# Transposing the second piece of v by DMA in a fused attention and FFN kernel, with later loads of w3, finer first folds and a split last piece of k

One core of a Trainium2 chip (trn2). The metric is the time of one execution in microseconds on the device; lower is better. The span that a profile shows is about 1.8 us less than that time.

## The reference

```python
# q, k, v: (4, 5824, 256) float32; tau = 1; w1, w2: (256, 1024); w3: (1024, 1024); w_out: (1024, 256)
qn = q / (norm(q, axis=1) + 1e-6)
kn = k / (norm(k, axis=1) + 1e-6)
s  = kn.transpose(0, 2, 1) @ qn / tau            # a 256 x 256 score matrix for each batch
a  = softmax(s)
x  = (v @ a).reshape(23296, 256)
h  = (x @ w1) * (x @ w2) @ w3
out = h @ w_out
```

## The kernel before

The kernel folds the softmax matrix into w1 and w2 for each batch (`Wf`), and w3 with w_out into one matrix `W` once. What is left for each batch is: for each chunk of 512 tokens and each of 8 slices j, products a and b (of `Wf` with the transposed v), `as` (ACT's copy of a), `abs = as * b` (VectorE), and o (TensorE, `abs` with `W`). TensorE works in program order here (below it stands for 3.4 us in front of chunk 6, with o products behind it that it could have run). While `W` isn't there yet, only a, b and `abs` run, and the `abs` wait in buffers: the 16 of chunks 0 and 1 in four free q buffers, the rest in a pool of 34.

```python
    def transpose_piece(n, pi):                     # by DMA, SBUF to SBUF, on SP's queue
        ...
        nc.sync.dma_start_transpose(vT[:, pi * PIECE : (pi + 1) * PIECE, :, :], t[:, :, :])

    def gate():                                     # POOL waits until VectorE is as far as this
        nc.gpsimd.tensor_copy(gate_t, last_ab[0][:1, :1])
    def hold(src):                                  # POOL waits until src is written; it issues all loads
        nc.gpsimd.tensor_copy(gate_t, src)

    # in emit_ab: where abs goes
            if b == 0 and c < 2:
                if j % 4 == 0:
                    held[0] = in_pool.tile([P, 4, 512], BF16, tag="q", ...)
                ab = held[0][:, j % 4, :]
            else:
                ab = work.tile([P, 512], BF16, tag="ab_sb", ..., bufs=8 * NDEF + 2)     # 34

    # loads of batch 0, in order
    load_piece("k", 0, 5)
    ...
    load_piece("q", 0, 5, (1, 3, 4)); load_part("v", 0, 0, 0, half)
    # w1 and w2 in three steps, then
    load_part("v", 0, 0, half, PIECE); load_piece("v", 0, 1); load_piece("v", 0, 2)
    nc.gpsimd.dma_start(out=wout_sb, ...)
    nc.gpsimd.dma_start(out=w3_bf, in_=w3r)

    # the agenda of batch 0: at(time on TensorE's own clock, its cost, what)
            at(4.6, 0.5, lambda: transpose_half_on_pe(0, 0, 1, False))
            at(7.0, 0.5, lambda: transpose_half_on_pe(0, 1, 0, True))      # v piece 1, on TensorE
            at(8.0, 0.5, lambda: transpose_half_on_pe(0, 1, 1, False))
            at(15.0, 0.0, transpose_w3)                                    # four DMA transposes
            at(15.0, 0.0, lambda: transpose_piece(0, 2))
            for jt in range(FT):
                at(27.5 + 1.2 * jt, 0.87, lambda jt=jt: w_unit(jt))
            moves = [("qk", 1, 0, 29.0), ("v", 0, 3, 30.0), ("v", 0, 4, 30.5), ("qk", 1, 1, 44.0), ...]
            t0, t1 = 54.0, 113.0                    # the score units of batch 1 lie between these
```

## Time and profile before

| | kernel before |
|---|---|
| time, median of 6 runs | 569.5 us (569.38 to 569.57) |
| span of the profiled run, mean granted TensorE clock | 567.7 us, 0.999 |
| TensorE busy | 557.6 us, 98% |
| first product a | 37.27 us |
| chunk 2, chunk 6 begin (need v pieces 1 and 3) | 55.4, 106.6 us |
| waits of TensorE after the first a | none |

How to read the views: PE is TensorE (PEld its weight loads), DVE is VectorE, ACT ScalarE, POOL GpSimd and SP SyncE; a timeline line of SPq or POOL with a DMA shows the issue of transfers, not their landing. A wait line says who waited, for whom, and then the total in us, the number of times and the longest. A timeline line has start and length in us, the engine, the line of the kernel, the operation, and in brackets how long the engine had been idle and what ended that. Line numbers differ by one or two between the kernels.

### The profile page before, as it was taken

To read this page: it belongs to the slowest core of one execution; us is meant where nothing else is said; L and a number is where in the kernel's file an instruction comes from. 1 tells how busy PE (TensorE), PEld (TensorE's weight loads), DVE (VectorE), ACT (ScalarE), POOL (GpSimd) and SP (SyncE) were. 2 spreads that over 40 slices of the span, in tenths; PEclk is the share of its full clock that TensorE was granted. 3 is DMA by queue.
4 is the path that set the end of the run, shared out by engine and by line. 5 is a ranking of instruction groups with operands and counts; after the bars stand their busy time and mean duration, and the time that the engine had idled before them with its cause. 6 is when DMAs were issued, how large, how long until landed. Compare 5 with 4: busy or idle time off the path is not lost.

```text
span 567.7 us, 10095 instructions
## 1 busy us (share of the span) xinstructions
PE 557.6 (98%) x3755; PEld 355.4 (63%) x3755; DVE 375.4 (66%) x581; ACT 338.7 (60%) x627; POOL 77.9 (14%) x163
## 2 busy tenths in 40 slices
PE   8799999999999999999999999999999999999997
PEld 5664566776656666666656566666655655665655
DVE  1047645888966577888766668787876665565564
ACT  1057536777766577777675567777765554454453
POOL 4260013120111111121210101030120000000000
PEclk9999999999999999999999999999999999999999
DMA  9999989978455796595661595765740325221011
GB/s 213 211 182 209 173 171 237 226 164 192 115 142 121 143 192 148 90 193 123 145 149 75 97 219 117 155 120 121 185 112 39 85 74 149 64 68 71 38 70 61
DMA packets 75104, 77.45 MB, mean 136 GB/s; under 512 B 54192, under 2 KB 58800, under 8 KB 75056
## 3 DMA queue, kind: packets, MB, share of 16 engines
q0 software_dynamic: 15760, 38.93, 39.3%
q1 hardware_dynamic: 59008, 37.23, 22.0%
q10 hardware_dynamic: 288, 0.66, 0.4%
q8 instruction: 29, 0.48, 0.3%
q14 instruction: 19, 0.16, 0.1%
HBM read 78.91 MB, written 23.86 MB: 181 GB/s over the span
## 4 chain that ended last, share of the span: by engine, by line
PE 93%; DMA 5%; ACT 1%; POOL 0%; issue 0%; DVE 0%; ACTq 0%; POOLq 0%
PE o L521 28%; PE b L476 28%; PE a L476 28%; PE G L192 5%; DMA k<-in_k_dram 5%; PE fold L363 2%; PE w L649 1%; ACT kr L283 0%; PE quarter L389 0%; POOL k L111 0%; POOL q L111 0%; PE sqk L225 0%; PE row L271 0%; ACT e L322 0%; ACT Wf L398 0%
## 5 line engine op out<-in xcount | busy, mean ns | idle before, releaser
L497 DVE TENSOR_TENSOR abs<-as,b 128x512 bf16<-128x512 bf16 x336 | 230.6, 687 | 143.9 <-ACT as L482 131.4
L482 ACT CAST as<-a 128x512 bf16<-128x512 f32 (+1 forms) x384 | 215.9, 562 | 170.4 <-DVE abs L497 84.7
L476 PEld LDWEIGHTS <-Wf 128*128 128x128 bf16 x1536 | 149.0, 98 | 102.3 <-ACT Wf L398 0.6
L476 PE MATMUL a<-vT,Wf 128*128 128x512 bf16 x704 | 209.6, 379 | 0.4 <-ACT Wf L398 0.4
L476 PE MATMUL b<-vT,Wf 128*128 128x512 bf16 x704 | 209.6, 379 | 0.0
L521 PE MATMUL o<-W_sb,abs 128*128 128x256 bf16 x1344 | 201.5, 273 | 0.0
L521 PEld LDWEIGHTS <-abs 128*128 128x128 bf16 x1344 | 131.2, 98 | 79.8 <-issue 0.2
L201 DVE TENSOR_TENSOR acc<-acc,sq 128x1024 f32<-128x1024 f32 x66 | 80.4, 1219 | 0.6 <-ACT sq L189 0.6
L192 PE MATMUL G<-k,q 128*128 128x256 bf16 x276 | 49.8, 273 | 0.0
L189 ACT ACTIVATE sq<-q 128x512 f32<-128x512 bf16 x66 | 41.8, 633 | 0.0
L189 ACT ACTIVATE sq<-k 128x512 f32<-128x512 bf16 x66 | 41.5, 629 | 0.0
L464 POOL COPY gate_t<-abs 1x1 bf16<-1x1 bf16 x39 | 10.5, 269 | 171.7 <-DVE abs L497 168.8
L543 DVE COPY osb<-o 128x512 f32<-128x512 f32 x44 | 30.1, 685 | 0.9 <-PE o L521 0.9
L192 PEld LDWEIGHTS <-q 128*128 128x128 bf16 x276 | 27.0, 98 | 3.1
L542 ACT COPY osb<-o 128x512 f32<-128x512 f32 x44 | 25.8, 586 | 4.1 <-PE o L521 2.1
L468 POOL COPY gate_t<-vT 1x1 bf16<-1x1 bf16 x16 | 3.1, 193 | 158.8 <-DMA vT<-v 158.8
L111 POOL DMA_DIRECT2D q<-in_q_dram x28 | 15.1, 540 | 12.5 <-DMA k<-in_k_dram 5.5
L370 ACT ACTIVATE Wf<-fold,rs 128x512 bf16<-128x512 f32 x15 | 10.3, 687 | 10.9 <-PE fold L363 8.7
L283 ACT ACTIVATE kr<-row 128x256 f32<-128x256 f32 x1 | 0.4, 383 | 26.1 <-PE row L271 26.1
L363 PE MATMUL fold<-w,e 128*128 128x512 bf16 x56 | 15.0, 379 | 0.0
L487 DVE TENSOR_TENSOR left<-as,b 128x192 bf16<-128x192 bf16 x32 | 11.3, 354 | 5.1 <-ACT as L482 2.7
L497 DVE TENSOR_TENSOR abq<-as,b 128x512 bf16<-128x512 bf16 x16 | 10.8, 686 | 5.0 <-ACT as L482 4.5
(98 smaller groups left out, 242.3 us busy)
## 6 DMA issues: line engine op xcount, KB each, us to landing
out_dram<-osb SPq DMA_DIRECT2D x44, 512.0 KB, 3.3
k<-in_k_dram POOLq DMA_DIRECT2D x19, 512.0 KB, 8.3
v<-in_v_dram POOLq DMA_DIRECT2D x19, 512.0 KB, 5.2
q<-in_q_dram POOLq DMA_DIRECT2D x18, 512.0 KB, 5.8
w_wout<-in_moe_w_dram POOLq DMA_DIRECT2D x1, 2048.0 KB, 22.7
k<-in_k_dram POOLq DMA_DIRECT2D x4, 320.0 KB, 8.8
v<-in_v_dram POOLq DMA_DIRECT2D x4, 320.0 KB, 4.9
q<-in_q_dram POOLq DMA_DIRECT2D x3, 320.0 KB, 4.1
```

Source lines behind the costliest of these rows:

```text
L111: nc.gpsimd.dma_start(out=pieces[nm, n, pi][:, lo:hi, :], in_=qk_main[nm, n][0][:, pi * PIECE + lo : pi * PIECE + hi, :])
L189: nc.scalar.activation(out=dst[:, :, part, :], in_=src[:, o : o + 2, :], func=AF.Square)
L192: nc.tensor.matmul(G[:, ct, :], lhsT=qt[:, i, ct * P : (ct + 1) * P], rhs=kt[:, i, :], start=(pr == 0 and part == 0 and ct == 0), stop=(pr ...
L201: nc.vector.tensor_add(accs[n], accs[n], sqs[0])
L363: nc.tensor.matmul(m, lhsT=st["e"][:, c2, c1 * P : (c1 + 1) * P], rhs=w12[:, c2, w, lo:hi], start=(c2 == 0), stop=(c2 == CT - 1),)
L476: nc.tensor.matmul(t[:, :n], lhsT=Wf[b][:, ct, w, j * P : (j + 1) * P], rhs=rhs_of(b, c, ct), start=(ct == 0), stop=(ct == CT - 1),)
L482: nc.scalar.copy(a_sb[:, :n], tiles[0][:, :n])
L487: nc.vector.tensor_mul(both, a_sb[:, :n], tiles[1][:, :n])
L497: nc.vector.tensor_mul(ab, a_sb, tiles[1])
L521: nc.tensor.matmul(tl[h][:, o, :], lhsT=lhsT, rhs=W_sb[:, j, :], start=(j == 0 and o == 0), stop=(j == FT - 1 and (small or o == 1)), skip ...
L542: nc.scalar.copy(o[:, 0:2, :], tl[0])
L543: nc.vector.tensor_copy(o[:, 2:4, :], tl[1])
```

## The change

Its intent: take 16 transposes off the full TensorE (piece 1 of v goes by DMA, like the later pieces), and let the first a begin sooner (less work behind the last piece of k, smaller first folds). The DMA transposes of pieces 2 and 1 need the DMA engines to themselves, so w3 is held behind them, and W, the loads of batch 1 and the later v move back.

```diff
         def first_folds():
             sum_mm(0)
             for c1 in range(CT):
-                quarter_mm(0, c1, 0)              # 256 columns of w1 and w2 at a time
+                columns_mm(0, P, c1, 0)           # 128 columns
             sum_mm(1)
             for c1 in range(CT):
-                quarter_mm(0, c1, 1)
+                columns_mm(0, P, c1, 1)
+            for c1 in range(CT):
+                for c2 in range(CT):
+                    columns_mm(P, P, c1, c2)
 ...
-    load_piece("k", 0, 5)
+    load_piece("k", 0, 5, (half - 1,))
 ...
-    nc.gpsimd.dma_start(out=wout_sb, ...)         # now in load_w3()
-    nc.gpsimd.dma_start(out=w3_bf, in_=w3r)
 ...
-    squares("k", 5, range(LAST + 1), end=True)
+    squares("k", 5, [LAST, *range(half - 1)])
+    squares("k", 5, range(half - 1, LAST), end=True)
 ...
-            at(7.0, 0.5, lambda: transpose_half_on_pe(0, 1, 0, True))
-            at(8.0, 0.5, lambda: transpose_half_on_pe(0, 1, 1, False))
-            at(15.0, 0.0, transpose_w3)
-            at(15.0, 0.0, lambda: transpose_piece(0, 2))
+            at(0.0, 0.0, lambda: transpose_piece(0, 2))
+            at(0.0, 0.0, lambda: transpose_piece(0, 1))
+            at(0.0, 0.0, lambda: hold(vTs[0][0][:1, PIECE, 0, :1]))
+            at(0.0, 0.0, load_w3)
+            at(16.0, 0.0, transpose_w3)
             for jt in range(FT):
-                at(27.5 + 1.2 * jt, 0.87, lambda jt=jt: w_unit(jt))
-            moves = [("qk", 1, 0, 29.0), ("v", 0, 3, 30.0), ("v", 0, 4, 30.5), ("qk", 1, 1, 44.0), ("qk", 1, 2, 45.0)]
+                at(37.0 + 1.2 * jt, 0.87, lambda jt=jt: w_unit(jt))
+            moves = [("qk", 1, 0, 35.0), ("v", 0, 3, 35.5), ("qk", 1, 1, 49.0), ("qk", 1, 2, 51.0), ("qk", 1, 3, 55.0)]
 ...
-            t0, t1 = 54.0, 113.0
+            t0, t1 = 56.5, 114.0
 ...
-        before = (0, 2) if b == 0 else None       # what POOL's first hold waits for
+        before = "w3" if b == 0 else None         # now the last transpose of w3
```

More of the change, by code (lines that the diff above doesn't have):

```diff
@@ L378, in fold, with columns_mm @@
                 fold_mm((w, c1, h * 512, (h + 1) * 512), c2, tag, i % 2 == 0 or (n == 0 and i == 7))
-        def quarter_mm(lo, c1, c2):
+        def columns_mm(lo, width, c1, c2):
             if c2 == 0:
-                tag = "ab" if lo == 0 else "out"
+                tag = "ab" if lo < 256 else "out"
                 st[lo, c1] = psum.tile(
-                    [P, 2, 256], F32, tag=tag, name=f"quarter_{lo}_{c1}", bufs={"ab": 4, "out": 3}[tag]
+                    [P, 2, width], F32, tag=tag, name=f"columns_{lo}_{c1}", bufs={"ab": 4, "out": 3}[tag]
                 )
@@ L389, in quarter_mm @@
                 nc.tensor.matmul(
-                    m[:, w, :], lhsT=st["e"][:, c2, c1 * P : (c1 + 1) * P], rhs=w12[:, c2, w, lo : lo + 256],
+                    m[:, w, :], lhsT=st["e"][:, c2, c1 * P : (c1 + 1) * P], rhs=w12[:, c2, w, lo : lo + width],
                     start=(c2 == 0 and w == 0), stop=(c2 == CT - 1 and w == 1), skip_group_check=True,
@@ L393, in quarter_mm @@
             if c2 == CT - 1:
-                for o in (0, P) if lo == 0 else (slice(0, 256),):
-                    cols = slice(o, o + P) if lo == 0 else o
-                    dst, src = Wf[n][:, c1, :, lo : lo + 256][:, :, cols], m[:, :, cols]
-                    if c1 == 0:
-                        nc.scalar.activation(out=dst, in_=src, func=AF.Copy, scale=st["rs"][:, c1 : c1 + 1])
-                    else:
-                        nc.vector.tensor_scalar_mul(dst, src, st["rs"][:, c1 : c1 + 1])
+                dst = Wf[n][:, c1, :, lo : lo + width]
+                if c1 == 0:
+                    nc.scalar.activation(out=dst, in_=m, func=AF.Copy, scale=st["rs"][:, c1 : c1 + 1])
+                else:
+                    nc.vector.tensor_scalar_mul(dst, m, st["rs"][:, c1 : c1 + 1])
         def first_folds():
@@ L412, in second_quarter @@
                 for c2 in range(CT):
-                    quarter_mm(256, c1, c2)
+                    columns_mm(256, 256, c1, c2)
         if n == 0:
@@ L621 @@
     load_piece("v", 0, 2)
-    nc.gpsimd.dma_start(out=wout_sb, in_=moe_w_out.rearrange("(lh ll) c -> ll lh c", ll=P))
-    nc.gpsimd.dma_start(out=w3_bf, in_=w3r)
     squares("k", 4, whole)
@@ L658, in w_unit, with load_w3 @@
             w_ready[0] = True
+    def load_w3():
+        nc.gpsimd.dma_start(out=wout_sb, in_=moe_w_out.rearrange("(lh ll) c -> ll lh c", ll=P))
+        nc.gpsimd.dma_start(out=w3_bf, in_=w3r)
     def load_library():
@@ L675, in make_agenda @@
             at(4.6, 0.5, lambda: transpose_half_on_pe(0, 0, 1, False))
-            at(7.0, 0.5, lambda: transpose_half_on_pe(0, 1, 0, True))
-            at(8.0, 0.5, lambda: transpose_half_on_pe(0, 1, 1, False))
-            at(15.0, 0.0, transpose_w3)
-            at(15.0, 0.0, lambda: transpose_piece(0, 2))
-            for jt in range(FT):
-                at(27.5 + 1.2 * jt, 0.87, lambda jt=jt: w_unit(jt))
-            moves = [("qk", 1, 0, 29.0), ("v", 0, 3, 30.0), ("v", 0, 4, 30.5), ("qk", 1, 1, 44.0), ("qk", 1, 2, 45.0)]
-            moves += [("qk", 1, 3, 53.0), ("qk", 1, 4, 55.0), ("v", 0, 5, 61.0), ("qk", 1, 5, 73.0)]
-            moves += [("v", 1, 0, 88.0), ("v", 1, 1, 98.0), ("v", 1, 2, 120.0), ("qk", 2, 0, 130.0)]
-            t0, t1 = 54.0, 113.0
+            at(0.0, 0.0, lambda: transpose_piece(0, 2))
[3 more added lines that the diff above has]
+            at(16.0, 0.0, transpose_w3)
+            for jt in range(FT):
+                at(37.0 + 1.2 * jt, 0.87, lambda jt=jt: w_unit(jt))
+            moves = [("qk", 1, 0, 35.0), ("v", 0, 3, 35.5), ("qk", 1, 1, 49.0), ("qk", 1, 2, 51.0), ("qk", 1, 3, 55.0)]
+            moves += [("qk", 1, 4, 57.0), ("v", 0, 4, 60.0), ("qk", 1, 5, 80.0), ("v", 0, 5, 83.0)]
+            moves += [("v", 1, 0, 97.0), ("v", 1, 1, 106.0), ("v", 1, 2, 120.0), ("qk", 2, 0, 130.0)]
+            t0, t1 = 56.5, 114.0
         else:
@@ L691, in make_agenda @@
             t0, t1 = 16.0, 98.0
-        before = (0, 2) if b == 0 else None
+        before = "w3" if b == 0 else None
         for nm, m, pi, t in moves:
             if before is not None and not (nm == "v" and before == (m, pi - 1) == (0, 3)):
-                at(t, 0.0, lambda w=before: hold(vTs[w[0]][1][:1, 0, :1] if w[1] == NP_ - 1 else vTs[w[0]][0][:1, w[1] * PIECE, 0, :1]))
+                at(t, 0.0, lambda w=before: hold(w3T[-1][:1, 1, FT - 1, :1] if w == "w3" else vTs[w[0]][1][:1, 0, :1] if w[1] == NP_ - 1 else vTs[w[0]][0][:1, w[1] * PIECE, 0, :1]))
             at(t, 0.0, gate)
```

## The prediction

> **What bounds the kernel now.** I read the page's busy shares first, then who TensorE waited for, before and after its first product of v, then the chain that ended last in order of time, and last the issuing engines of the first 110 us, because the change is mostly about transfers.
>
> ```profile
> PE 557.6 (98%) x3755; PEld 355.4 (63%) x3755; DVE 375.4 (66%) x581; ACT 338.7 (60%) x627; POOL 77.9 (14%) x163
> ```
> From the waits of PE, stretch 0 to 37.5 us, then 37.5 us to the end:
> ```profile
> PE sqq L225 <- DMA q<-in_q_dram: 3.6, 3, 1.7
> ...
> PE a L476 <- ACT Wf L398: 0.4, 1, 0.4
> ```
> ```profile
> PE a L476 <- ACT Wf L398: 0.4, 1, 0.4
> ```
> In the first 37 us TensorE waits for q and k and for the softmax. After that it waits for nothing: the one 0.4 us wait listed is the first product itself, which ends the start. So from 37.3 us to the end every TensorE microsecond removed is a microsecond of span, and every new wait of TensorE is one too. The chain in order of time (start us, us, what) shows the places that the change touches:
> ```profile
> 15.74 14.71 DMA k<-in_k_dram
> ...
> 30.50 0.84 PE sqk L225 x12
> ...
> 36.74 0.48 ACT Wf L398
> 37.22 0.05 issue
> 37.27 0.60 PE a L476 x2
> ...
> 44.88 0.45 PE tr_I-615_616 L134 x8
> ...
> 46.19 0.45 PE tr_I-635_636 L134 x8
> ...
> 65.76 0.87 PE w L649 x8
> ```
> The end of the last k piece, the first fold, two groups of PE transposes of v piece 1, and the first W unit are all on the path. Counting pairs a, b in this chain by eights gives when each chunk starts: chunk 2 (the first that needs piece 1) at 55.40, chunk 4 (piece 2) at 76.20, chunk 6 (piece 3) at 106.60, chunk 8 at 139.2.
>
> The transfers behind it: the queue of SP in order of time, then POOL's, then the issues of two short windows, each of which catches one transfer (KB, us from issue to landing):
> ```profile
> 59.49 9.41 SPq L574 DMA_TRANSPOSE w3T<-w_wout  x4
> ...
> 68.95 2.35 SPq L157 DMA_TRANSPOSE vT<-v  x1
> ...
> 83.81 5.10 SPq L157 DMA_TRANSPOSE vT<-v  x2
> ```
> ```profile
> 36.69 0.97 POOL L623 DMA_DIRECT2D w_wout<-in_moe_w_dram  x1
> ...
> 72.99 0.18 POOL L468 COPY gate_t<-vT 1x1 bf16<-1x1 bf16 x1 [34.80 <-DMA vT<-v]
> ...
> 73.73 0.60 POOL L111 DMA_DIRECT2D q<-in_q_dram  x1 [0.33 <-PE w L649]
> ...
> 74.97 0.53 POOL L111 DMA_DIRECT2D v<-in_v_dram  x1
> ```
> ```profile
> v<-in_v_dram POOLq DMA_DIRECT2D x1, 512.0 KB, 11.6
> ```
> ```profile
> w_wout<-in_moe_w_dram POOLq DMA_DIRECT2D x1, 2048.0 KB, 22.7
> ```
> Piece 2 of v lands at 35.29 + 11.6 = 46.9, w_out at 49.5, w3 at 36.69 + 22.7 = 59.4; its four transposes run at once, the last landing 11.6 us later at 71.1; the transpose of v piece 2 lands at 72.95; that releases POOL, which issues q, k, v piece 3. Piece 3 lands at 74.97 + 8.8 = 83.8, its transpose 5.3 us later at 89.1. Chunk 6 wants it at 106.60: 17.5 us to spare.
>
> **What the Trainium skill says.** "TensorE: Matmul & The Clock Gate", section "Back-to-back issue gap", gives N/2.4 + 2.5 ns for an isolated warm matmul, but 81 ns for a sustained stream at N=128. This trace agrees with the former: 0.45 us for 8 transposes is 56 ns each, and two 512-column matmuls take 0.43. Its Part 1 says the clock halves after an idle window of about 3.4 us; in this trace waits up to 1.7 us left matmuls at full speed, so I expect a stall under 3 us to cost itself only. "DMA: Bandwidth & Descriptors", section "Issuing engines are not separate DMA queues", says that all issuers share 16 engines. So a DMA transpose is not free for the loads; in the kernel before, the v piece 3 transpose beside a load took 5.3 us to land and the following one, alone, 3.9. Its "Latency and other measured facts" gives 261 GB/s for a transpose; here two 512 KB transposes land 1.9 us apart, 276 GB/s.
>
> **The change part by part.**
>
> *PE transposes of v piece 1.* 16 matmuls in two groups of 0.45 us are gone from a stretch where PE never waits: -0.90. Their two copies (1.01 us on ACT, 0.68 on DVE) were beside it: 0.
>
> *Last k piece in two parts.* Five of its six slots came in one transfer; now slots 0 to 2 are in the first part with the tail, and only slots 3 and 4 (4 of 12 matmuls) stand behind the last landing. 8 x 56 ns = 0.45 at most. Behind them in order is the first q part, which lands about 96 KB / 210 GB/s = 0.46 us after k, so some of it is lost: -0.35.
>
> *First folds by 128.* Only 4 matmuls of 128 columns, not of 256, precede the second sum and again the first scaling: TensorE reaches both earlier, but the second exponential (ends 36.09) and the reciprocal (36.64) come in between. The wait of ACT from 36.64 to 36.74 goes, and a little of the sum's: -0.12. The eight matmuls of columns 128 to 255 fit in the idle 0.4 us before product a. Later shares of w12 are issued perhaps 0.1 us later, since one more DMA stands in the queue: +0.05.
>
> Sum of the gains: 0.90 + 0.42 at the start (0.35 + 0.12 - 0.05) = 1.3 us, 0.23%.
>
> *The order of transfers.* This is what decides the sign. The program is in order: on SP, transposes of piece 2, piece 1, then w3; on POOL, w3's load waits for piece 1's transpose, and everything behind (q, k, v piece 3) for the last w3 transpose. Worked on:
> - piece 2 lands 46.9; its transpose, alone, about 4.0: 50.9; piece 1 follows 1.9 later: 52.8. Chunk 2 now starts at 55.40 - 0.90 - 0.42 = 54.1. It fits by about 1 us.
> - w3's loads are issued at 53.1; the first transfer after an idle stretch of the queue needs about 2.6 us more than its bytes (512 KB of q: 5.1, against 2.5 for each next one); w_out and w3 took 59.4 - 46.9 = 12.5 back to back. Landing 53.1 + 2.6 + 12.5 = 68.2 (59.4 before).
> - w3's transposes: + 11.6 = 79.8. The first is there at 72.5; W now begins behind 40 pairs of a, b, at 74.6. W's last pair of units wants the last transpose at about 83. It fits.
> - q, k, v piece 3 go out; before, piece 3 landed 10.8 after the release: 90.6. Its transpose, now alone, 3.8 instead of 5.3: 94.4.
> - chunk 6. Summing the durations of the new matmul order (each 512-column pair 0.433, each W unit or group of eight o matmuls 0.87) from the first a on, it starts at 92.6 with the old start (the missing transposes are in that sum already), and at 92.2 with the start 0.42 earlier. W moves behind one more chunk and fewer o products go ahead, so it is 14.4 us earlier than before.
> TensorE then stands for 94.4 - 92.2 = 2.2 us in front of chunk 6, in order, with o products behind it that can't pass.
> - Chunk 8 and piece 4: four q, k pairs go first, about 27.7 us from v piece 3's transpose to piece 4's landing (before: 26.5 for the same pairs and the 352 KB of piece 5), + 4.0. Chunk 8 comes 33.5 of TensorE time after chunk 6. It fits by some 2 us.
> Total: 569.5 - 1.3 + 2.2 = 570.4.
>
> **The rivals.**
> 1. *The transfers are in time, and only the gain shows.* Needs piece 3's transpose 2.2 us sooner: w3's transposes in 9 us, not 11.6 (SP's own gaps between them, 1.8 to 3.4 us, are uneven), or less start-up in the two loads behind waits. For it: the change puts W and the loads at hand-set times. Against it: four serial steps, each with a measured duration, and 17.5 us of slack that loses 14.4 to chunk 6's earlier place and 8.8 to w3's later landing, and wins back only 1.9 (piece 2's transpose is no longer behind w3) and 1.5. Time: 568.2.
> 2. *Chunk 2 stalls as well.* If piece 2's transpose takes 5.3 rather than 4.0 us, piece 1 is late by 0.3 and w3's whole train shifts by 1.3. Time: 571.5 to 572.
> 3. *A second stall at chunk 8,* if output stores add more than I allow: up to 1 us more. ACT and DVE don't become the bound: with 0.56 and 0.69 us for each pair of 0.866.
>
> **Range and chances.** All gains and no stall, with 0.3 more at the start, give 567.9; rival 2 gives 572. Both are inside 0.5%, while 2% is 11.4 us; nothing in the trace is that large, short of a stall that I have overlooked. 570.4, range 567.8 to 572.0; faster by 2%: 0.01, same 0.98, slower 0.01.
>
> **What would show it.** After: PE's chain has 8 rather than 24 transposes after the first a; the first a starts at 36.7 to 36.9; matmuls behind the last k landing number 4; PE waits at line 477 for the DMA into vT, once, 1.5 to 3.3 us, between 91 and 95; w3's first transpose starts near 68, q's load near 80.5. Step by step it is wrong if PE has no wait after the start (then rival 1 and a time near 568.2), if the wait stands near 54 (rival 2), or if matmuls after the stall run longer than 379 ns (clock).

## More of the kernel before

The main lines of before are in the prediction. One more is needed later, VectorE's waits from 90 to 125 us, where the o products catch up and the sums of squares of batch 1 run as well:

```profile
DVE abs L497 <- ACT as L482: 7.9, 10, 1.5
DVE acc L201 <- ACT sq L189: 0.6, 2, 0.4
DVE osb L543 <- PE o L521: 0.4, 2, 0.2
```

VectorE waits briefly and often for its inputs, and never long for anything else.

## The result

The changed kernel took 574.88 us in the median of 6 runs (571.76 to 577.05), the kernel before 569.5. The ratio is 1.0091 (95% interval 1.0064 to 1.0118): slower by 0.9%, outside the stated range of 567.8 to 572.0, though within 2% as forecast. Ratios here and below are the mean time of one kernel's fast runs over that of the other's of the same rounds, so not quite the ratio of the medians quoted. The spread is new: 5.3 us between runs, where the kernel before has 0.2 (0.4 to 1.5 in the later rounds), and the times go with the mean granted TensorE clock (577.05 at 0.992, four runs of 574.65 to 574.98 at 0.997, 571.76 at 0.999). The profile is of the slowest of these runs; its span is 575.3 us, 7.6 more than before.

The waits of TensorE, over the whole span (the lines above 0.5 us that before doesn't have):

```profile
PE a L477 <- DMA vT<-v: 3.4, 1, 3.4
...
PE columns L389 <- DMA w<-in_moe_w_dram: 0.7, 1, 0.7
```

The predicted wait at line 477 is there, 3.4 us where 2.2 were worked out. The train of transfers behind it, from SP's queue and then POOL's in order of time, and the issue line of w3:

```profile
47.56 3.77 SPq L157 DMA_TRANSPOSE vT<-v  x2
71.17 7.65 SPq L575 DMA_TRANSPOSE w3T<-w_wout  x4
92.75 1.59 SPq L157 DMA_TRANSPOSE vT<-v  x1
```
```profile
53.33 0.18 POOL L469 COPY gate_t<-vT 1x1 bf16<-1x1 bf16 x1 [16.61 <-DMA vT<-v]
...
54.50 0.90 POOL L662 DMA_DIRECT2D w_wout<-in_moe_w_dram  x1
81.02 0.18 POOL L469 COPY gate_t<-w3T 1x1 bf16<-1x1 bf16 x1 [25.62 <-DMA w3T<-w_wout]
...
82.96 0.54 POOL L111 DMA_DIRECT2D v<-in_v_dram  x1
```
```profile
w_wout<-in_moe_w_dram POOLq DMA_DIRECT2D x1, 2048.0 KB, 16.6
```

Piece 1 is transposed by 53.3, w3 lands at 54.50 + 16.6 = 71.1, its transposes by 81.0, v piece 3 at 92.7, its transpose at 96.4. TensorE had been ready at 93.1. What follows is what the prediction did not expect, though it named it as a sign of being wrong: matmuls slower than 379 ns after the stall. The chain that ended last, then TensorE's clock in stretches of 2 us (busy us and number of instructions of PE, PEld, DVE, ACT, POOL, then the granted clock, the DMA share and GB/s):

```profile
82.96 9.77 DMA v<-in_v_dram
92.73 0.02 issue
92.75 3.68 DMA vT<-v
96.43 0.05 issue
96.47 1.04 PE a L477 x2
97.51 0.85 PE b L477 x2
98.36 1.71 PE o L522 x8
```
```profile
92.00:94.00 2.00, 1.10 (x10) 0.68 (x7) 1.38 (x2) 1.00 (x2) 0.00 (x0) 1.00 0.03 6
94.00:96.00 2.00, 0.00 (x0) 0.00 (x0) 0.00 (x0) 0.00 (x0) 0.00 (x0) 0.89 1.27 311
96.00:98.00 2.00, 1.52 (x4) 0.59 (x5) 0.00 (x0) 0.45 (x1) 1.08 (x4) 0.50 0.51 209
98.00:100.00 2.00, 2.00 (x10) 1.35 (x9) 0.69 (x1) 0.66 (x2) 1.67 (x5) 0.50 0.70 94
100.00:102.00 2.00, 2.00 (x8) 0.78 (x7) 0.00 (x0) 0.61 (x2) 0.00 (x0) 0.50 1.02 205
102.00:104.00 2.00, 2.00 (x15) 1.46 (x14) 0.69 (x1) 0.59 (x2) 0.26 (x1) 0.91 1.06 217
```

b takes 0.85 us where it took 0.43, eight o 1.71 where they took 0.87: after the pause TensorE ran at half clock for almost 6 us. PE's busy share shows nothing of it, it is 98% in both kernels, because slow matmuls count as busy.

My account of the 7.6 us, from the profiled runs, is: the wait 3.4; the half clock about 3.0 (from 96.5 to 102.2 at half speed); the wait for w1 and w2 0.7; and two losses that stand in no wait line of that size, about 0.7 each, which the experiments name below. Against it stand -0.24 at the first a and -0.90 for the transposes. The sum is 7.4; 0.2 I can't place. The start of one of the two losses shows in VectorE's waits from 90 to 125 us, where the kernel before (above) has no such line; the experiments say what it waits for:

```profile
DVE abs L498 <- PE o L522: 6.2, 1, 6.2
```

The other shows at the end of batch 0: its last small matmuls lose 0.7 us there.

### The profile page after: what moved, and what is told of

The parts are those of the page before. It is cut to its first block, busy times and chain, and to the rows that moved or that the text cites. A ratio compares the mean times of both kernels' runs of the same rounds, so it can differ in the third digit from the quotient of the medians.

```text
span 575.3 us, 10087 instructions
## 1 busy us (share of the span) xinstructions
PE 562.1 (98%) x3747; PEld 357.2 (62%) x3747; DVE 374.6 (65%) x580; ACT 337.8 (59%) x626; POOL 82.0 (14%) x166
## 4 chain that ended last, share of the span: by engine, by line
PE 88%; DMA 9%; POOL 1%; DVE 1%; issue 0%; ACT 0%; POOLq 0%; DVEq 0%; ACTq 0%
PE o L522 27%; PE a L477 27%; PE b L477 27%; PE G L192 5%; DMA q<-in_q_dram 3%; PE fold L363 2%; DMA v<-in_v_dram 2%; DMA k<-in_k_dram 1%; DMA w<-in_moe_w_dram 1%; DMA w3T<-w_wout 1%; DMA vT<-v 1%; DVE acc L201 0%; POOL q L111 0%; POOL w L618 0%; POOL k L111 0%
## 5 line engine op out<-in xcount | busy, mean ns | idle before, releaser
L469 POOL COPY gate_t<-vT 1x1 bf16<-1x1 bf16 x17 | 5.5, 322 | 155.5 <-DMA vT<-v 155.5
L111 POOL DMA_DIRECT2D q<-in_q_dram x28 | 15.1, 540 | 18.4 <-PE o L522 7.1
L363 PE MATMUL fold<-w,e 128*128 128x512 bf16 x56 | 15.2, 379 | 0.0
L111 POOL DMA_DIRECT2D k<-in_k_dram x25 | 13.7, 550 | 7.5 <-DMA k<-in_k_dram 3.5
## 6 DMA issues: line engine op xcount, KB each, us to landing
w_wout<-in_moe_w_dram POOLq DMA_DIRECT2D x1, 2048.0 KB, 16.6
```

The costliest lines, as they stand in the source:

```text
L111: nc.gpsimd.dma_start(out=pieces[nm, n, pi][:, lo:hi, :], in_=qk_main[nm, n][0][:, pi * PIECE + lo : pi * PIECE + hi, :])
L363: nc.tensor.matmul(m, lhsT=st["e"][:, c2, c1 * P : (c1 + 1) * P], rhs=w12[:, c2, w, lo:hi], start=(c2 == 0), stop=(c2 == CT - 1),)
```

## The experiments

Eleven runs were made (ten kernels, and the changed one again), in three groups, each group on one chip with its own runs of the kernel before (medians 569.3, 569.47, 569.45). All gave correct results. The theory was that the pause before chunk 6 costs itself and the clock; the rivals were contention, VectorE catching up, and transfers that are late for other reasons.

**Fill the pause.** Fourteen useless matmuls (3.0 us) where TensorE stood still:

```diff
                 run_due()
+                if (b, c, j) == (0, 6, 0):
+                    busy(14)
                 emit_ab(b, c, j)
```

> The changed kernel with 14 useless 512-column matmuls (3.0 us at 216 ns) put ahead of the first product of chunk 6, where TensorE stood still for 3.4 us. Theory A (the pause lets the clock fall to half for some 6 us, which costs about 3 us more than the pause and makes the runs differ): a wait of only 0.3 to 0.6 us is left, granted clock 0.998 or more in every run, 571.6 to 572.0 in every run, so 3 us less than the changed kernel's median of 574.9. Theory B (the rest is lost to late transfers or to VectorE catching up after the stall): no change, 574.5 to 575.5, and spread as before.

573.41 us (573.31 to 573.47; 4 runs with a mean clock of 0.999 or 1.0), ratio 1.0068 (1.0053 to 1.0083). TensorE's wait, the filler in its timeline, and the stretch that had run at half clock:

```profile
PE a L477 <- DMA vT<-v: 0.6, 1, 0.6
```
```profile
91.92 3.18 PE L213 MATMUL warm_I-1197_1198<-warm 128*128 128x512 bf16 x14
95.72 0.61 PE L477 MATMUL a<-vT,Wf 128*128 128x512 bf16 x2 [0.62 <-DMA vT<-v]
```
```profile
94.00:98.00 4.00, 3.38 (x22) 1.87 (x20) 0.69 (x1) 1.11 (x2) 1.83 (x6) 1.00 0.81 219
```

More work made the kernel 1.5 us faster in the medians (1.3 against the kernel before of each round), and the spread shrank from 5.3 us to 0.16. So the half clock after the pause costs time. That it also makes the spread fits, but isn't shown to be all of it: the run with the last k piece whole, below, spreads by 2.8 us with a clock of 0.999 or 1.0 in every run. The size was missed: I expected 3 us, the clock loss of the profiled run, which was the slowest; a median run lost 0.3% of its clock, 1.7 us. And 573.4, not 571.8, is left, so a full clock and a pause of 3.6 us don't explain all of the loss.

**v piece 3 first.** It is loaded ahead of q and k of batch 1, not behind:

```diff
-            moves = [("qk", 1, 0, 35.0), ("v", 0, 3, 35.5), ...
+            moves = [("v", 0, 3, 34.5), ("qk", 1, 0, 35.0), ...
```
(The hold for piece 3's transpose stays where it was, ahead of q and k piece 1.)

> The changed kernel with v piece 3 loaded ahead of q and k of batch 1 instead of behind them. Theory A (piece 3 is 3.4 us late because 1 MB of q and k stands ahead of it): it lands 5 us sooner, near 87, its transpose near 92, chunk 6 waits for nothing, clock stays full: 568.3 to 569.2. Rival (the train is late as a whole, and the wait moves to q and k of batch 1 or to chunk 8): a PE wait for q, k or vT of 1 us or more, 570 or above.

574.23 us (573.71 to 574.42; clocks 0.995 to 0.997), ratio 1.0081 (1.0066 to 1.0096). The forecast failed by 5 us. The chain and TensorE's clock around it:

```profile
85.68 8.90 DMA vT<-v
94.58 0.05 issue
94.63 1.03 PE a L477 x2
```
```profile
93.00:94.00 1.00, 0.00 (x0) 0.00 (x0) 0.00 (x0) 0.00 (x0) 0.00 (x0) 1.00 1.29 313
94.00:95.00 1.00, 0.37 (x1) 0.13 (x2) 0.00 (x0) 0.00 (x0) 0.23 (x2) 0.53 1.02 408
95.00:96.00 1.00, 1.00 (x4) 0.42 (x3) 0.00 (x0) 0.30 (x1) 0.69 (x3) 0.50 0.15 57
```

Piece 3 did land 7 us sooner, at 85.7. But its transpose now ran beside the 1 MB of q and k and took 8.9 us, where alone it had taken 3.7. The gain was lost beside that load. The pause became 2.6 us, and that was enough to halve the clock.

**The same with the last k piece whole,** as in the kernel before (`load_piece("k", 0, 5)` and one `squares` call).

> As the run with v piece 3 first, and the last k piece in one transfer again (four of twelve matmuls no longer ahead). Theory A (the extra transfer takes one of eight places in flight, holds back q's last parts and then w12, so that the second folds wait 0.7 us and v lands 0.6 us later): the wait of the second folds is gone, the first a starts 0.05 to 0.15 us later, 0.5 us faster than with k split: 567.9 to 568.6. Rival (the split is worth its place): equal or up to 0.4 us slower than with the split.

571.9 us (569.95 to 572.78; clocks 0.999 and 1.0), ratio 1.0037 (1.001 to 1.0064). Faster by 2.3 us, not by 0.5, and not for the expected reason: neither this run nor the one above shows the 0.7 us wait for w1 and w2. What differs is the pause, and with it the clock:

```profile
93.95 0.60 PE L477 MATMUL a<-vT,Wf 128*128 128x512 bf16 x2 [1.73 <-DMA vT<-v]
```
```profile
94.00:95.00 1.00, 1.00 (x6) 0.51 (x7) 0.00 (x0) 0.40 (x1) 0.60 (x3) 1.00 1.03 426
```

TensorE reached chunk 6 0.2 us later and the piece was there 0.7 us sooner (its transpose took 8.2 us), so the pause was 1.7 us, and after it the clock stayed at 1.00. Between 1.7 and 2.6 us of pause lies the difference between a cost of the pause and a cost of the pause plus the clock; the last experiment narrows this. Whether the split of k causes the wait for w1 and w2 this can't tell: of the ten profiles of kernels with the split, two show that wait or its like (the changed one and the next below) and eight don't, among them the changed kernel's second profile, so it isn't there in every execution.

**w3 early again.** w_out and w3 are loaded right behind v piece 2, as before the change, with no hold.

> The changed kernel with w3 and w_out loaded right behind v piece 2, as in the kernel before, without waiting for piece 1's transpose; W and all moves stay where the change put them. Theory A (the wait of w3's load for the transpose of piece 1 makes everything behind it some 11 us later): w3 lands near 60, v piece 3's transpose near 85, no wait at chunk 6. The two transposes now run beside the load: piece 1 is ready at 54.5 to 57, chunk 2 (54.8) may wait up to 2 us: 568.5 to 571. Rival (only the order v behind q and k matters): the wait at chunk 6 stays over 2 us.

582.31 us (581.94 to 583.54), ratio 1.0228 (1.0212 to 1.0245), much worse than either theory had it. SP's queue and TensorE's wait:

```profile
47.49 14.88 SPq L157 DMA_TRANSPOSE vT<-v  x2
```
```profile
PE a L477 <- DMA vT<-v: 10.0, 1, 10.0
```
```profile
vT<-v SPq DMA_TRANSPOSE x1, 15.2
```

The first transpose took 15.2 us from issue to landing beside the load of w3 (4.0 in the changed kernel, alone), and chunk 2 waited 10.0 us for piece 1. This shows why the change holds w3 back: the delay of everything behind is the price of two DMA transposes, which need the DMA engines to themselves for about 6 us.

**The two small parts alone,** each put into the kernel before: the folds by 128 columns, and the split of the last k piece.

> The kernel before with the first folds by 128 columns and nothing else. Prediction's step: 0.1 us faster at the start (the first a 0.1 to 0.2 us sooner after the exponential), 569.2 to 569.5 against 569.4. Rival (the second scaling of ACT and DVE now waits for its own matmuls and holds back the first a of unit 1): equal or 0.1 to 0.3 us slower.

569.63 us (569.34 to 570.01) against 569.47, ratio 1.0002 (0.9989 to 1.0014).

> The kernel before with the last k piece of batch 0 loaded and squared in two parts, nothing else. Prediction's step: 0.35 us faster. Rival (a ninth transfer in a window of eight holds back the issue of q's last parts, w12 and v by 0.3 to 0.6 us): the chain to the first a is no more than 0.1 us shorter, v lands 0.3 to 0.6 us later, and a wait of PE of up to 0.7 us for w12 or v appears: 569.4 to 570.1.

569.56 us (569.26 to 569.79) against 569.47, ratio 1.0002 (0.9988 to 1.0016), with no wait of TensorE for w1, w2 or v.

Neither is visible in the time; the intervals are 0.7 us and more wide on each side, so effects of 0.1 and 0.35 us are neither shown nor excluded. In the profiles, the folds shorten the way from the first sum to the first a from 1.52 us (35.75 to 37.27) to 1.43 (36.02 to 37.45). Ten profiles of kernels with the split have their first a at 36.6 to 37.4, mean 36.8; three without it have 37.0 to 37.5, mean 37.2. The difference of 0.4 is of the size predicted, with the spread of each as large or larger. (The latest of each group, 37.4 and 37.5, come from profiles in which the clock was low from about 19.5 to 22.9 us.)

**v piece 3 in the train of w3.** It is loaded directly behind w3 and transposed directly behind w3's transposes, while no load runs; q and k of batch 1 follow. (The 5.5 puts its load behind the PE transpose at 4.6, the last to read the v buffer that it takes.)

```diff
     def load_w3():
         nc.gpsimd.dma_start(out=wout_sb, ...)
         nc.gpsimd.dma_start(out=w3_bf, in_=w3r)
+        load_piece("v", 0, 3)
 ...
-            at(0.0, 0.0, lambda: hold(vTs[0][0][:1, PIECE, 0, :1]))
-            at(0.0, 0.0, load_w3)
+            at(5.5, 0.0, lambda: hold(vTs[0][0][:1, PIECE, 0, :1]))
+            at(5.5, 0.0, load_w3)
             at(16.0, 0.0, transpose_w3)
+            at(16.0, 0.0, lambda: transpose_piece(0, 3))
-            moves = [("qk", 1, 0, 35.0), ("v", 0, 3, 35.5), ("qk", 1, 1, 49.0), ...
+            moves = [("qk", 1, 0, 35.0), ("qk", 1, 1, 49.0), ...
-        before = "w3" if b == 0 else None
+        before = (0, 3) if b == 0 else None
```

> The changed kernel with v piece 3 loaded directly behind w3, in the same train, and transposed directly behind w3's transposes with no load in flight; q and k of batch 1 go out after that. Theory A (chunk 6 waits because piece 3 is loaded and transposed last, and its transpose is slow only beside a load): piece 3's transpose lands near 83, no wait for vT, clock 0.999 or more, runs within 0.5 us of each other: 568.7 to 569.9. Rival (some other loss of the change remains, as a late W or q and k): over 571.

569.69 us (569.55 to 570.09; clocks 0.998 to 1.0), ratio 1.0004 (0.9992 to 1.0017), as expected. SP's queue:

```profile
69.99 8.06 SPq L575 DMA_TRANSPOSE w3T<-w_wout  x4
78.16 1.94 SPq L157 DMA_TRANSPOSE vT<-v  x1
```

The transpose of piece 3 landed at 82.2, ten microseconds ahead of need, the wait for vT and the slow clock were gone, and 5.2 us with them. But the kernel only equals the one before, though it has 0.9 us less TensorE work. Something still took back about 1 us. VectorE's timeline of this run shows one place:

```profile
95.16 0.69 DVE L498 TENSOR_TENSOR abs<-as,b 128x512 bf16<-128x512 bf16 x1 [1.27 <-ACT as L483]
101.78 0.69 DVE L498 TENSOR_TENSOR abs<-as,b 128x512 bf16<-128x512 bf16 x1 [5.93 <-PE o L522]
102.39 1.22 DVE L201 TENSOR_TENSOR acc<-acc,sq 128x1024 f32<-128x1024 f32 x1
```

A product that reads `as` and b waits for an o, 5.9 us long. No o feeds it; it wants a place to write. With W some 9 us later, all 34 product buffers were full, and the first 16 o products only free the q buffers. VectorE then had to make up for its rest together with the sums of squares, and was the bound for some microseconds (TensorE's waits for `osb` and `as`, 0.3 and 0.2 us, are its echo). A second place is the last chunk of batch 0 near 175 us, whose matmuls have only 192 columns: TensorE's starts there fall 0.7 us behind its full speed. In the kernel before the folds of batch 1 begin 9 us ahead of that chunk, here 5.

**The folds earlier.** The same kernel with `t1` at 112 rather than 114.

> As the run before this one, and the score units of batch 1 spread over 2 us less, so that the folds of batch 1 begin 7 us ahead of the last small chunk of batch 0 rather than 5 (9 in the kernel before). Theory: the 0.7 us that TensorE lost among the small matmuls of the last chunk comes back, 0.4 to 0.8 us faster than without: 568.0 to 569.2, so faster than the kernel before. Rival (VectorE, now denser in the score stage, becomes the bound there): equal or slower.

570.08 us (569.71 to 570.3), ratio 1.001 (0.9997 to 1.0022): the rival fits, though the ranges of the two kernels overlap. The loss at the last chunk was gone, but near 110 us TensorE lost 1.0 us to a denser VectorE.

**Room for the products.** The kernel with v piece 3 in the train, and the products of chunk 2 in two v buffers that are free by then:

```diff
-            if b == 0 and c < 2:
+            if b == 0 and c < 3:
                 if j % 4 == 0:
-                    held[0] = in_pool.tile([P, 4, 512], BF16, tag="q", ...)
+                    tag = "q" if c < 2 else "v"
+                    held[0] = in_pool.tile([P, 4, 512], BF16, tag=tag, ...)
```

> As the run with v piece 3 in the train of w3, and the eight products of chunk 2 of batch 0 kept in two freed v buffers, so that 42 rather than 34 + 16 - 8 of the later ones find room before W is there (58 in all, 50 before). Theory (VectorE stood still for 5.9 us from 95.9 to 101.8 because all 34 product buffers were full until the first o of such a buffer, and the products and sums of squares it then had to make up held back TensorE by 0.75 us): VectorE's wait for o near 96 to 102 is gone, PE's waits for ACT near 105 and 110 too, 0.5 to 0.9 us faster than 569.7: 568.8 to 569.2. Rival (the loss near 105 comes from the density of score units alone): no change, 569.5 to 569.9.

(The numbers of places in that text are muddled; what is meant is 58 places instead of 50.) 569.0 us (568.87 to 569.5), ratio 0.9993 (0.998 to 1.0006), in the medians 0.7 us faster than without the room, as expected. VectorE's waits from 90 to 125 us are those of the kernel before again:

```profile
DVE abs L499 <- ACT as L483: 7.6, 8, 1.5
DVE acc L201 <- ACT sq L189: 0.7, 2, 0.4
DVE osb L545 <- PE o L523: 0.4, 1, 0.4
```

**Both.** Room and `t1` at 112:

> As the run before this one, and the score units of batch 1 over 2 us less. Theory (the two losses, full product buffers and late folds at the last small chunk, are separate and add): 0.6 to 0.8 us faster again, 568.1 to 568.6, so 0.9 to 1.4 us faster than the kernel before, which is what the removed transposes and the earlier start are worth. Rival (VectorE remains the bound in the score stage): 569.0 to 570.

568.43 us (568.15 to 569.06) against 569.45, ratio 0.9984 (0.9972 to 0.9996). It beats the kernel before by 1.0 us in the medians, and the changed kernel by 6.6. With room, the earlier folds are worth 0.6 us in the medians; without it they had cost 0.4 (the ranges overlap in both pairs, so the sizes are rough). No run put the room and the earlier folds into the kernel before, so it isn't shown that the 1.0 us comes from the transposes and the start alone. All waits of TensorE that are left lie in the start:

```profile
PE sqq L225 <- DMA q<-in_q_dram: 3.5, 3, 1.7
PE warm_I-92_93 L213 <- DVE warm L78: 1.2, 1, 1.2
PE sum L340 <- ACT e L322: 0.4, 1, 0.4
PE sqk L225 <- DVE k L582: 0.2, 1, 0.2
```

**The changed kernel again,** unaltered.

> The changed kernel unaltered, once more, for the spread of its runs beside their clock. Theory (pause of TensorE before chunk 6, and the clock falls after it in most runs, not in all): most runs at 574 to 577 with a mean granted clock of 0.992 to 0.997, any run at 0.999 or more at 571 to 573.5. Rival (the spread has another cause): no order between clock and time.

575.03 us (572.0 to 576.36), ratio 1.0089 (1.0071 to 1.0108). By run, time and clock: 574.81 at 0.995, 576.36 at 0.989, 572.0 at 0.998, 575.26 at 0.997, 575.25 at 0.995, 573.6 at 1.0. The slowest run has the lowest clock and the two fastest the highest, so the order is there, though 572.0 at 0.998 lies below 573.6 at 1.0: the runs also differ by a microsecond or so in something else, perhaps the pause itself, of which only profiled runs tell.

**What the profiles say of the clock.** At the start TensorE waits for q, and in two profiles such a wait lay close to the limit: the split of k alone, and the folds by 128 columns alone.

```profile
19.00 1.07 PE L225 MATMUL sqq<-q 128*128 128x128 bf16 x16 [2.09 <-DMA q<-in_q_dram]
```
```profile
19.33 1.77 PE L225 MATMUL sqq<-q 128*128 128x128 bf16 x16 [2.23 <-DMA q<-in_q_dram]
```

After 2.09 us of idle time the sixteen matmuls ran at full speed. After 2.23 us they took longer: the granted clock stood at 0.50 from 19.5 to 22.9 us (the same after 2.32 us in the run with the folds earlier). In the second profile of the changed kernel the clock fell only 1.2 us after TensorE had resumed from a pause of 3.5 us, at 96.6, and was back at 100.1. Low stretches lasted 3.4 us in four profiles, 6.8 in the first profile of the changed kernel, and 10.2 with w3 early: whole multiples of 3.4 us. So the cost comes in steps and isn't set by the length of the pause alone. Two profiles of one kernel, with pauses of 3.4 and 3.5 us, lost about 3.0 and 1.7 us to it. A clock that is set anew every 3.4 us, wherever the pause falls, would fit this; no run was made to test it.

## Why the prediction was wrong

- **The bound** was right: every microsecond of wait after 37 us went into the span.
- **The gains** (1.3 us) were about right. With the losses taken away, the kernel is 1.0 us faster than before (with the reservation made there). The transposes' 0.90 is read from the chain; the 0.35 and 0.12 of the start agree with the profiles but not beyond their spread. The 0.05 for w1 and w2 was too low in the profiled run (a wait of 0.7), and what decides when that happens stays open.
- **The wait at chunk 6** had its place and mechanism right and its size 1.2 us short: 3.4 instead of 2.2. Term by term: w3 landed at 71.1, not 68.2. I had taken 12.5 us from one landing to the next, in a queue that was running, and added 2.6 for the start; from POOL's release to the landing it was 17.8, not 15.1. Its transposes took 9.8, not 11.6; q, k and v piece 3 took 11.7 from the release, not 10.8. Together the piece was there at 96.4, not 94.4. TensorE was there at 93.1, not 92.2.
- **"I expect a stall under 3 us to cost itself only"** is the step that failed. The pause grew to 3.4 us, but the step was wrong below 3 as well: 2.6 us halved the clock in the run with piece 3 first, and 2.2 and 2.3 us did at the start of two others. The waits of up to 1.7 us in the kernel before, from which I argued, could not show where the limit lies. The clock's cost was about 3 us in the profiled run and 1.3 to 1.5 in the median; the filler run shows it.
- **"ACT and DVE don't become the bound"** failed too. I compared VectorE's 0.69 us with TensorE's 0.866 for each pair, but didn't count the places for its results: moving W by 9.5 us on TensorE's clock lets 11 more pairs pile up. That, and the folds that came later against the last chunk, cost 0.7 and 0.6 us by the last experiments. Together: 570.4 + 1.2 (longer wait) + 1.5 (clock) + 1.3 (these two) = 574.4, where 574.88 was measured.
- **The rivals.** The first (transfers in time, 568.2) describes the repaired kernel, at 568.4. The second (chunk 2 stalls as well) didn't happen in the changed kernel. It did, at 10 us, as soon as w3 was loaded beside the transposes, and for the reason that I had read from the trace (5.3 against 3.9 us beside a load) and thought smaller. The third was not seen.
- **A citation.** The 261 GB/s is what "DMA: Bandwidth & Descriptors" gives for a transpose with a non-contiguous middle dimension; the prediction leaves that out, and no sum rests on it.

## What to carry to other kernels

When work leaves a full engine by way of a DMA transpose, count the time in which no load may run beside it, and follow everything that this delays up to the next thing that the full engine needs. Moving the start of a consumer back needs buffers for what piles up ahead of it; a producer's wait for its own consumer in the profile is the sign that there are too few. A pause of a full TensorE of more than some 2 us should be priced with what follows it at half clock, and the granted clock in short stretches shows this where busy shares don't.

## What the Trainium skill lacked or had wrong

- "TensorE: Matmul & The Clock Gate", Part 1, has the clock halved after an idle window of about 3.4 us, and its table of advice warns of gaps above about 3 us. Here pauses of 2.2, 2.3 and 2.6 us were enough (the clock then stood at 0.50), and 1.7 to 2.1 us were not. The length of the window agrees: low stretches lasted 3.4, 6.8 and 10.2 us.
- The same page, "Back-to-back issue gap", gives 81 ns for each matmul of 128 columns and 131 ns for 512 in a sustained stream with weight loads. These kernels, with a weight load for each matmul (3755 of both in the kernel before), sustain 56 and 216 ns, its formula for an isolated one.
- "DMA: Bandwidth & Descriptors", "Rules for kernel authors", says that a transpose next to ordinary DMAs "needs nothing". That holds for correctness in all eleven runs. How much longer it then takes the page doesn't say: a 512 KB transpose took 3.7 to 4.0 us alone, 8.9 beside 1 MB of loads and 15.2 beside the load of w3.
